# Key-maxima units of a gated attention kernel: four single PSUM banks each, 92 instead of 76 of them in the front

## The chip, the core and the metric

The kernel runs on one core of one Trainium2 chip. TensorE (PE in the profile) multiplies matrices into PSUM, a memory of eight banks of 128 partitions by 512 fp32 values. ScalarE (ACT) and VectorE (DVE) read PSUM and SBUF, GpSimd (POOL) works on SBUF, and SyncE's queue (SP) issues the transfers. Each engine executes its own instructions in the order in which they are written, and waits on semaphores for the others. The metric is the device time of one execution in microseconds; the figure given is the median over runs.

## The reference

`x` is 2048 tokens of 448 features, 16 heads of 28. Branch A is a linear attention with learned softmax features, branch B a full softmax attention; a gate per token mixes them.

```python
def _A_ref(x, wqkv, w_phi, wo):
    qkv = (lambda x, *d: x.transpose(*d))((x @ wqkv).reshape(B, S, 3, H, Dh), 2, 0, 3, 1, 4)
    q, k, v = qkv[0], qkv[1], qkv[2]
    pq = jnp.einsum("bhsd,hdf->bhsf", q, w_phi)
    pk = jnp.einsum("bhsd,hdf->bhsf", k, w_phi)
    phi_q = jnp.concatenate([_softmax(pq, axis=-1), _softmax(-pq, axis=-1)], axis=-1)
    phi_k = jnp.concatenate([_softmax(pk, axis=-1), _softmax(-pk, axis=-1)], axis=-1)
    kv = jnp.einsum("bhsf,bhsd->bhfd", phi_k, v)
    z  = jnp.einsum("bhsf->bhf", phi_k)
    num = jnp.einsum("bhqf,bhfd->bhqd", phi_q, kv)
    den = jnp.einsum("bhqf,bhf->bhq", phi_q, z)[..., None] + 1e-6
    ...
def _B_ref(x, wqkv, wo):
    ...
    scores = jnp.einsum("bhqd,bhkd->bhqk", q, k) * scale
    p = _softmax(scores, axis=-1)
    o = jnp.einsum("bhqk,bhkd->bhqd", p, v)
    ...
g = _sigmoid((x * gate_w).sum(-1, keepdims=True))
return g * a + (1 - g) * b
```

## The kernel before

The kernel is one long program whose order on PE, DVE, ACT and POOL is the order of the Python code (`manual_schedule`, L52). It has two parts.

**The front** (up to about 360 us) computes the projections of both branches, all of branch A, and the values of branch B. After a first stretch of query and key projections (`first_units`, `proj_qk`), one loop (L712) runs over steps `i`, with `t = i` counting key tiles of 128 tokens of branch A for the first 16 steps, and `q = i - 16` counting query tiles and what follows them. A step with a key tile runs eleven matmuls of keys (`pk`), eleven of values (`pva`), the features (`features1`, `features2`: on DVE two reductions `ext`, the sum `fsum` and a reciprocal per tile; the exponential on ACT; subtractions and a multiplication on POOL) and every second step `kv_add` for two tiles, 32 small matmuls that the trace shows as 64. The steps from `q = 18` on (the value stage) run `value_b`, eleven matmuls `pvb` for 128 tokens of branch B's values, and `out_a`, twelve matmuls `poa`. After the loop, `value_b` runs on for value tiles 8 to 15 (L887).

**The attention** (L1129) takes 256 steps: a step is one block of 512 queries, one tile of 128 keys and four heads. Per step it runs four score matmuls `st` (L856), four exponentials `p` on ACT (L872), and eight matmuls `pv` of the values (L1000). Steps 1 to `first` go in pairs (n = 2), later ones up to `LAST` = 232 singly, then in pairs again.

**The maxima.** The softmax of branch B subtracts a bound, the greatest score of each query and head, which must be known before that query block's attention. The whole task is `NU` = 256 units of four matmuls. `NF` = 76 of them run in the front as `mx_unit`; the rest run in the attention as `mx_visit`, one per pair or per single step, so `first = 2 * (LAST - len(flats) // 4)` follows from `NF`: 180 visits are left, the first 104 steps go as 52 pairs with one visit each, and steps 105 to 232 have one visit each.

A front unit (L260) works on 128 queries, two heads and two blocks of 512 keys. Four matmuls of 28 rows, in the four row quarters of the array, make for each head scores of one block (into `pmb`) and the difference of the two blocks' scores (into `pmd`). The greater of two numbers is one plus the relu of their difference: ACT takes the relu of `pmd` (both heads, 128x1024) into `rl`, then DVE adds `pmb` to `rl` and takes the maximum, one instruction for each head (L291). `pmb` and `pmd` are tiles of two banks each. Their pool has four banks (`mx`, two buffers of two banks) until the loop ends; then a new layout (`psv`, L882) has two single banks for the projections and six for the units.

Where units stand in the front: four in the last projections (L669); in the key tiles one at the start of every second step (L718) and three more after counted matmuls (`pace`, `tick`, L704); one in each of the steps q = 0, 1 and from q = 8 on (L757); one more just ahead of `value_b` for 19 <= q < 26 (L803); the rest spread evenly over value tiles 8 to 14 (L891). The differences of key blocks that units need come with `pair_load` (SP transfers, then a subtraction on POOL, taken by `take_subs`).

Of the kernel before, what the change touches and what calls it, by code (L numbers as in the profile page):

```python
# [8 lines left out]
F32 = mybir.dt.float32  # L9
F32R = mybir.dt.float32r  # L10
U32 = mybir.dt.uint32
AF = mybir.ActivationFunctionType
ALU = mybir.AluOpType
# [13 lines left out]
SCALE = DH ** -0.5  # L27
EPS = 1e-6
NU = NG * NQ * 16
NF = 76  # L30
LOWEST = -3.0e38
LAST = 232
OUTS = (200, 238, 246, 206)
# [8 lines left out]
def gated_mix_kernel(ctx, tc, xT, wqkB, wvB, wvA, wkAT, wqAT, phi, woA, woB,  # L42
# [15 lines left out]
    ps = ps_s_.enter_context(tc.tile_pool(name="ps", bufs=1, space=PSUM, reuse_waits="tile"))  # L58
    dr = ctx.enter_context(tc.tile_pool(name="dr", bufs=1, space=DRAM))

    psn = [3, 2]

    def ps_s(nm):
        return ps.tile([P, 512], F32, tag="s", name=nm, bufs=psn[0])
# [1 line left out]
    def ps_pv(nm):  # L66
        return ps.tile([P, 512], F32, tag="pv", name=nm, bufs=1)

    def ps_mx(nm, d):
        return ps.tile([P, 2, 512], F32, tag="md" if d and psn[1] == 3 else "mx", name=nm,  # L70
                       bufs=1 if d and psn[1] == 3 else 2)


    def scratch(nm, shape):
# [185 lines left out]
    def mx_unit():  # L260

        u = mxs["u"]
        if u == NF:
            return
        mx_fin()
        take_diffs(2)
        mxs["u"] = u + 1
        gq, r = divmod(u, 16)
        g, qb = divmod(gq, NQ)
        if gq < GM:  # L270
            c, qt = divmod(r, 4)
            hp, b = divmod(c, 2)
            col = 64 * gq + 16 * b + 4 * qt + 2 * hp
            if r in (4, 9):
                pair_query(gq + 1, r // 9)
        else:
            c, qt = divmod(r, QM)
            hp, b = divmod(c, 2)
            col = 64 * gq + 4 * QM * b + 4 * qt + 2 * hp
            if r == 0:  # L280
                mx_query(gq)
        qc, kc = mxs[("qp", gq, hp)], mxs[("kp", g, c)]
        pb, pd = ps_mx(f"pmb{u}", False), ps_mx(f"pmd{u}", True)
        for j in range(4):
            js = slice(32 * j, 32 * j + DH)
            nc.tensor.matmul((pb if j < 2 else pd)[:, j % 2, :], qc[js, qt * P:(qt + 1) * P],  # L286
                             kc[js, :], start=True, stop=True, tile_position=(32 * j, 0))
        rl = rlp.tile([P, 2, 512], F32, tag="rl", name=f"rl{u}", bufs=2 if psn[1] == 3 else 1)
        nc.scalar.activation(rl, pd, AF.Relu)  # L289
        for i in range(2):  # L290
            nc.vector.tensor_tensor_reduce(rl[:, i, :], pb[:, i, :], rl[:, i, :], 1.0, LOWEST,  # L291
                                           ALU.add, ALU.max, part[:, col + i:col + i + 1])
        if gq < GM and qt == 3 and qb == NQ - 1:
            pair_load(g + 1, c)
        if gq == GM and qt == QM - 1:
            mx_load(g, c)
        if r == 15:
            mx_reduce(gq)
# [312 lines left out]
    def first_units():  # L611
# [5 lines left out]
            nc.sync.dma_start(raw[b][:, 1, :], xT[:, b, :512])  # L617
        x_loads(1)
        pqs = [ps_s(f"pqk0_{m}") for m in range(3)] + [ps_pv("pqk0_3")]
        pr = [ps_mx(f"pqk_{i}", False) for i in range(2)]  # L620
        later.extend((pr[0][:, 0, :], pr[1][:, 0, :], pr[0][:, 1, :]))
        for _ in range(8):
            nc.tensor.matmul(pqs[3][:, :P], ident, ident, start=True, stop=True)
        for b in range(4):
# [87 lines left out]
    for i in range(2 * NT + 11):  # L712
# [4 lines left out]
        if t < NT and t % 2 == 0:  # L717
            mx_unit()  # L718
            passes = (55 if t < NT - 4 else 44) + (4 if t >= 4 else 0)
            pace["n"], pace["at"] = 4 if t >= 4 else 0, [k * passes // 4 for k in (1, 2, 3)]  # L720
        if q in (0, 1):
            take_exps()

# [40 lines left out]
        if 2 <= q - 1 < NT:  # L764
            fq[q - 1] = features2(fq[q - 1], f"q{q - 1}")
        take_subs()
        if t == 1:
            pair_load(0, 3)
        if y >= 8 and y % 2 == 0 and tb - 4 < 8:
            num[tb - 4] = normalize3(*num[tb - 4], 2)  # L770
# [30 lines left out]
            turn(y - 2)  # L801
        if NT + 3 <= q < NT + 10:
            mx_unit()  # L803
        if q == NT + 2:
            bd_s.close()
            vb = [value_tile(0)]
        if 0 <= q - NT - 2 < 8:
            value_b(q - NT - 2)
        if y >= 5 and y % 2 and tb - 2 < 8:
            num[tb - 2] = normalize2(ta, *num[tb - 2], f"a{tb - 2}", 2, True)  # L810
    ta_s.close()
# [38 lines left out]
    def scores(s, i, js=range(4)):  # L850

        gq, kt = divmod(s, NT)
        g, qb = divmod(gq, NQ)

        def score(j, st):
            nc.tensor.matmul(st, kst_of[(g, kt // 4)][:, j, (kt % 4) * P:(kt % 4 + 1) * P],  # L856
                             qst_of[gq][:, j, :], start=True, stop=True)

        if s == 0:
            p = at.tile([P, 2, 512], F32, name=f"p{s}_{i}")  # L860
            st = ps_mx(f"st{s}_{i}", i)
            for jl in range(2):
                score(2 * i + jl, st[:, jl, :])
            nc.scalar.activation(p, st, AF.Exp, scale=SCALE)
            pts.setdefault(s, []).extend([p[:, 0, :], p[:, 1, :]])
            return
        sts = {j: bank(b, f"st{s}_{j}") for j, b in zip(js, i)}
        for j in js:
            score(j, sts[j])
        for j in js:  # L870
            p = late_p.tile([P, 512], F32, tag="p", name=f"p{s}_{j}", bufs=12)
            nc.scalar.activation(p, sts[j], AF.Exp, scale=SCALE)  # L872
            pts.setdefault(s, []).append(p)
# [4 lines left out]
    stg = at  # L878
    load_q(0)
    load_nm(0)  # L880
    ps_s_.close()
    ps = ps_s_.enter_context(tc.tile_pool(name="psv", bufs=1, space=PSUM, reuse_waits="tile"))  # L882
    psn[:] = 2, 3
    rlp = fr_s.enter_context(tc.tile_pool(name="rlp", bufs=1, reuse_waits="tile"))
    mx_unit()
    rest = NF - mxs["u"]
# [26 lines left out]
        return ps2.tile([P, 512], F32, tag=f"g{i}", name=nm, bufs=1)  # L913


    for i in (3, 4, 1, 2, 5, 6, 0, None):
        if i is None:
            ps2.tile([P, 512], F32, tag="pv", name="pv_first", bufs=1)
        else:
            bank(i, f"first{i}")  # L920
# [331 lines left out]
```

## Time and profile before

| | before |
|---|---|
| median of 3 runs (lowest, highest) | 1015.66 us (1015.43, 1016.14) |
| profiled execution, its own time | 1016.56 us |
| span of its trace | 1014.8 us |
| front, from 0 to the first attention matmul | 360.0 us |
| attention in pairs, first visit to last pair's visit | 366.5 to 593.8 us |
| attention singly | 593.8 to 924.4 us |
| granted TensorE clock | 1.000 |

Times in the trace are microseconds from the start of the span. In a timeline a row gives the start, the length from the first start to the last end of like instructions that follow each other, the engine, the line, the operation, output <- inputs, the shape, and how many there were. PE's ends are modelled and overlap, so the distance between starts on PE is read rather than the lengths. L110, L128 and L286 are the lines that issue projection and unit matmuls.

### The profile page before, as it was taken

What the parts mean: (1) busy time and instruction counts of PE and PEld (TensorE: products, weight loads), DVE (VectorE), ACT (ScalarE), POOL (GpSimd) and SP (SyncE); (2) the same over time, 40 slices, a digit from 0 to 9 for tenths busy, and PEclk for the clock granted to TensorE, in tenths of its full rate; (3) what the DMA queues carried; (4) which work ended last, traced back from release to release, by engine and by line L of the source; (5) the groups of instructions that cost most, each with busy time, mean ns of one, the idle gap of its engine ahead of it and who ended that gap; (6) DMA issues with size and microseconds to landing.
All of it is one profiled execution on the core that took longest, in us unless ns stands there. A gap on an engine that the chain in (4) does not pass through costs nothing.

```text
span 1014.8 us, 17693 instructions
## 1 busy us (share of the span) xinstructions
PE 1004.8 (99%) x6344; PEld 566.7 (56%) x6344; DVE 647.5 (64%) x1335; ACT 818.1 (81%) x1534; POOL 250.9 (25%) x218
## 2 busy tenths in 40 slices
PE   8999999999999999999999999999999999999998
PEld 7777877777777754444444443333333333335665
DVE  5467767898765535445444568888888788885112
ACT  5355655577765699999999999999999999997662
POOL 1225435578734820220110120110110101100010
PEclk9999999999999999999999999999999999999999
DMA  8874010113233671223542233342232247310441
GB/s 294 289 250 120 33 52 31 43 37 95 84 97 98 153 164 38 58 66 74 112 96 72 71 90 81 79 105 56 73 85 61 71 98 200 96 38 30 136 145 55
DMA packets 64570, 99.62 MB, mean 98 GB/s; under 512 B 18134, under 2 KB 24902, under 8 KB 64482
## 3 DMA queue, kind: packets, MB, share of 16 engines
q1 hardware_dynamic: 64482, 98.49, 35.8%
q8 instruction: 50, 0.82, 0.4%
q14 instruction: 38, 0.31, 0.1%
HBM read 70.29 MB, written 27.78 MB: 97 GB/s over the span
## 4 chain that ended last, share of the span: by engine, by line
PE 95%; DVE 3%; ACT 1%; DMA 1%; issue 0%; POOL 0%; DVEq 0%; ACTq 0%; POOLq 0%
PE st L856 28%; PE pv L1000 24%; PE pm L323 8%; PE pqk L110 5%; PE poa L110 4%; PE pk L128 4%; PE pva L128 4%; PE pmb L286 3%; PE pob L110 3%; PE pq L110 2%; PE pvb L110 2%; PE pvb L128 2%; PE pn L538 1%; PE pqk L640 1%; PE pft L526 1%; DVE featq L453 1%
## 5 line engine op out<-in xcount | busy, mean ns | idle before, releaser
L872 ACT ACTIVATE p<-st 128x512 f32<-128x512 f32 x1020 | 525.1, 639 | 26.4 <-PE st L856 26.4
L335 DVE TENSOR_REDUCE part<-pm 128x1 f32<-128x512 f32 x405 | 258.8, 685 | 178.7 <-PE pm L323 178.7
L856 PE MATMUL st<-qst,kst 128*128 128x512 f32 x1024 | 299.5, 422 | 0.1
L1000 PE MATMUL pv<-p,vb 128*32 128x512 f32 x2048 | 259.7, 601 | 0.0
L856 PEld LDWEIGHTS st<-qst,kst 128*128 128x128 f32 x1024 | 171.0, 187 | 101.6 <-ACT p L872 39.3
L425 POOL TENSOR_TENSOR oUb<-oUb,rsb 128x512 f32<-128x512 f32 x15 | 19.3, 1289 | 492.4 <-DMA rsb<-rdb 360.1
L291 DVE CUSTOM_DVE_ANT_0 rl<-pmb,rl 128x512 f32<-128x512 f32 x152 | 98.3, 684 | 57.0 <-ACT rl L289 57.0
L327 ACT ACTIVATE rl<-pm 128x512 f32<-128x512 f32 x180 | 111.5, 620 | 10.4 <-PE pm L323 10.0
L323 PEld LDWEIGHTS pm<-kc,qc 28*128 28x128 f32 x720 | 34.4, 181 | 150.9 <-ACT p L872 102.3
L289 ACT ACTIVATE rl<-pmd 128x1024 f32<-128x1024 f32 x76 | 78.1, 1028 | 38.2 <-PE pmd L286 31.0
L1000 PEld LDWEIGHTS pv<-p,vb 128*32 128x32 f32 x2048 | 50.5, 108 | 96.0 <-issue 93.6
L332 DVE CUSTOM_DVE_ANT_0 rl<-pm,rl 128x512 f32<-128x512 f32 x135 | 92.0, 681 | 0.0
L323 PE MATMUL pm<-kc,qc 28*128 28x512 f32 x720 | 91.2, 495 | 0.0
L110 PE MATMUL pqk<-XH,wB 128*128 128x512 f32 x192 | 59.6, 397 | 1.7 <-DVE ev L578 1.7
L577 ACT CAST ev<-pqk 128x512 fp32r<-128x512 f32 x28 | 15.9, 588 | 36.7 <-PE pqk L110 32.0
L110 PE MATMUL poa<-woA_s,oTa 128*128 128x448 f32 x192 | 43.4, 375 | 0.0
L110 PEld LDWEIGHTS pqk<-XH,wB 128*128 128x128 f32 x192 | 35.3, 188 | 10.6 <-DVE ev L578 2.2
L1011 DVE SCALAR_TENSOR_TENSOR acc<-pob,gate,acc 128x448 f32<-128x448 f32 x12 | 8.2, 684 | 50.8 <-PE pob L110 50.8
L128 PE MATMUL pk<-wkA_s,XH 128*128 128x448 f32 x128 | 39.5, 382 | 0.0
L286 PE MATMUL pmd<-kp,qp 28*128 28x512 f32 x152 | 38.0, 496 | 0.8 <-DVE part L291 0.8
L110 PEld LDWEIGHTS poa<-woA_s,oTa 128*128 128x128 f32 x192 | 34.9, 188 | 6.2 <-issue 3.2
L128 PE MATMUL pva<-wvA_s,XH 128*128 128x450 f32 x128 | 37.8, 371 | 0.0
(155 smaller groups left out, 1196.1 us busy)
## 6 DMA issues: line engine op xcount, KB each, us to landing
qkd<-ev SPq DMA_DIRECT2D x28, 512.0 KB
qst<-qkd SPq DMA_DIRECT2D x64, 224.0 KB
kst<-qkd SPq DMA_DIRECT2D x64, 224.0 KB
od<-oTb SPq DMA_DIRECT2D x48, 112.0 KB
rsa<-rda SPq DMA_DIRECT2D x8, 512.0 KB
rsb<-rdb SPq DMA_DIRECT2D x15, 256.0 KB
gad<-ga SPq DMA_DIRECT2D x16, 224.0 KB
acc<-gad SPq DMA_DIRECT2D x4, 896.0 KB
```

What stands on the lines that cost most here:

```text
L110: nc.tensor.matmul(dst, l, r, start=i == 0, stop=i == len(todo) - 1)
L128: nc.tensor.matmul(dst[:, :n], l, r, start=i == 0, stop=i == len(todo) - 1, skip_group_check=True)
L286: nc.tensor.matmul((pb if j < 2 else pd)[:, j % 2, :], qc[js, qt * P:(qt + 1) * P], kc[js, :], start=True, stop=True, tile_position=(32 * ...
L289: nc.scalar.activation(rl, pd, AF.Relu)
L291: nc.vector.tensor_tensor_reduce(rl[:, i, :], pb[:, i, :], rl[:, i, :], 1.0, LOWEST, ALU.add, ALU.max, part[:, col + i:col + i + 1])
L323: nc.tensor.matmul(pm[j], mxs[("qc", gq)][js, qt * P:(qt + 1) * P], mxs[("kc", g, kb)][js, :], start=True, stop=True, tile_position=(32 * ...
L327: nc.scalar.activation(rl, pm[kb], AF.Relu if kb < 3 else AF.Copy)
L332: nc.vector.tensor_tensor_reduce(r, pm[j], r, 1.0, LOWEST, ALU.add, ALU.max, part[:, col + j:col + j + 1])
L335: nc.vector.tensor_reduce(part[:, col + j:col + j + 1], pm[j], AX.X, ALU.max)
L856: nc.tensor.matmul(st, kst_of[(g, kt // 4)][:, j, (kt % 4) * P:(kt % 4 + 1) * P], qst_of[gq][:, j, :], start=True, stop=True)
L872: nc.scalar.activation(p, sts[j], AF.Exp, scale=SCALE)
L1000: nc.tensor.matmul(pv[32 * j:32 * j + 32, :], vb[kt // 8][:, kt % 8, 4 * g + j, :], pt[j], start=kt == 0, stop=kt == NT - 1, tile_position ...
```

## The change

A unit takes four single banks in place of two tiles of two, all from one tag `mx` with four buffers (six in the later layout). The matmuls of the differences are issued first, then those of the scores. Each head has its own relu of 128x512 and its own `rl` tile, and its DVE instruction follows. The pace in the key tiles asks for five places to two key tiles (matmul counts at fifths, not quarters). A third unit comes inside `value_b` for 19 <= q < 26, ahead of its sixth matmul. The layout `psv` is opened in step q = 22 (`NT + 6`), not after the loop. `NF` is 92. The load of the fourth pair of key blocks moves from step 1 to step 0. The first attention step takes four single banks and four exponentials of 128x512, and the order in which the attention's banks are laid out at its start is another one.

```diff
-NF = 76
+NF = 92
...
-    psn = [3, 2]
+    psn = [3, 4, 2]
...
-    def ps_mx(nm, d):
-        return ps.tile([P, 2, 512], F32, tag="md" if d and psn[1] == 3 else "mx", name=nm,
-                       bufs=1 if d and psn[1] == 3 else 2)
+    def ps_mx(nm):
+        return ps.tile([P, 512], F32, tag="mx", name=nm, bufs=psn[1])
...
-        pb, pd = ps_mx(f"pmb{u}", False), ps_mx(f"pmd{u}", True)
+
+        pm = [ps_mx(f"pm{'ddbb'[j]}{u}_{j % 2}") for j in range(4)]
         for j in range(4):
-            js = slice(32 * j, 32 * j + DH)
-            nc.tensor.matmul((pb if j < 2 else pd)[:, j % 2, :], qc[js, qt * P:(qt + 1) * P],
-                             kc[js, :], start=True, stop=True, tile_position=(32 * j, 0))
-        rl = rlp.tile([P, 2, 512], F32, tag="rl", name=f"rl{u}", bufs=2 if psn[1] == 3 else 1)
-        nc.scalar.activation(rl, pd, AF.Relu)
+            i = (j + 2) % 4
+            js = slice(32 * i, 32 * i + DH)
+            nc.tensor.matmul(pm[j], qc[js, qt * P:(qt + 1) * P], kc[js, :], start=True, stop=True,
+                             tile_position=(32 * i, 0))
         for i in range(2):
-            nc.vector.tensor_tensor_reduce(rl[:, i, :], pb[:, i, :], rl[:, i, :], 1.0, LOWEST,
-                                           ALU.add, ALU.max, part[:, col + i:col + i + 1])
+            rl = rlp.tile([P, 512], F32, tag="rl", name=f"rl{u}_{i}", bufs=psn[2])
+            nc.scalar.activation(rl, pm[i], AF.Relu)
+            nc.vector.tensor_tensor_reduce(rl, pm[2 + i], rl, 1.0, LOWEST, ALU.add, ALU.max,
+                                           part[:, col + i:col + i + 1])
...
-            pace["n"], pace["at"] = 4 if t >= 4 else 0, [k * passes // 4 for k in (1, 2, 3)]
+            pace["n"], pace["at"] = 4 if t >= 4 else 0, [k * passes // 5 for k in range(1, 5)]
...
-        if t == 1:
+        if t == 0:
             pair_load(0, 3)
...
+        if q == NT + 6:
+            ps_s_.close()
+            ps = ps_s_.enter_context(tc.tile_pool(name="psv", bufs=1, space=PSUM, reuse_waits="tile"))
+            psn[:2] = 2, 6
...
-            value_b(q - NT - 2)
+            value_b(q - NT - 2, lambda i: mx_unit() if i == 5 and q >= NT + 3 else None)
...
-            p = at.tile([P, 2, 512], F32, name=f"p{s}_{i}")
-            st = ps_mx(f"st{s}_{i}", i)
-            for jl in range(2):
-                score(2 * i + jl, st[:, jl, :])
-            nc.scalar.activation(p, st, AF.Exp, scale=SCALE)
-            pts.setdefault(s, []).extend([p[:, 0, :], p[:, 1, :]])
+            for j in (2 * i, 2 * i + 1):
+                p, st = at.tile([P, 512], F32, name=f"p{s}_{j}"), ps_mx(f"st{s}_{j}")
+                score(j, st)
+                nc.scalar.activation(p, st, AF.Exp, scale=SCALE)
+                pts.setdefault(s, []).append(p)
...
-    ps_s_.close()
-    ps = ps_s_.enter_context(tc.tile_pool(name="psv", bufs=1, space=PSUM, reuse_waits="tile"))
-    psn[:] = 2, 3
...
-    for i in (3, 4, 1, 2, 5, 6, 0, None):
+    for i in (0, None, 1, 6, 5, 4, 3, 2):
```

More of the change, by code (lines that the diff above doesn't have):

```diff
@@ L619, in first_units @@
         pqs = [ps_s(f"pqk0_{m}") for m in range(3)] + [ps_pv("pqk0_3")]
-        pr = [ps_mx(f"pqk_{i}", False) for i in range(2)]
-        later.extend((pr[0][:, 0, :], pr[1][:, 0, :], pr[0][:, 1, :]))
+        later.extend(ps_mx(f"pqk_{i}") for i in range(3))
         for _ in range(8):
```

## The prediction

> **What bounds the kernel now.** I read the page's busy line and chain first.
>
> ```profile
> span 1014.8 us, 17693 instructions
> PE 1004.8 (99%) x6344; PEld 566.7 (56%) x6344; DVE 647.5 (64%) x1335; ACT 818.1 (81%) x1534; POOL 250.9 (25%) x218
> PE 95%; DVE 3%; ACT 1%; DMA 1%; issue 0%; POOL 0%; DVEq 0%; ACTq 0%; POOLq 0%
> ```
>
> PE sets the end nearly everywhere, so a unit moved from the attention to the front isn't hidden in idle time: it is paid there and saved here, and the two prices have to be compared. They come from the stages. The busy times by window, the first over the paired steps (from the first pair's visit to the last pair's), the second over the single ones:
>
> ```profile
> core 0: us, PE busy (x) PEld busy (x) DVE busy (x) ACT busy (x) POOL busy (x), PEclk, DMA share, GB/s
> 366.53:593.85 227.32, 227.32 (x1436) 104.37 (x1432) 109.41 (x222) 227.16 (x461) 25.62 (x26) 1.00 0.35 80
> 593.85:924.40 330.55, 330.55 (x2048) 126.82 (x2048) 270.41 (x544) 320.36 (x642) 31.80 (x29) 1.00 0.35 84
> ```
>
> 51 periods of a pair lie in the first, 227.3/51 = 4.457 us each; ACT is busy throughout, so the pairs run at the pace of ACT. The second holds 128 single steps (2048 matmuls, 16 each), 330.55/128 = 2.582 us each; ACT has 10 us of slack there, and PE sets the pace. ACT's own timeline shows the price of a pair, one relu and eight exponentials without a gap, 4.45 us from relu to relu:
>
> ```profile
> 469.69 0.60 ACT L327 ACTIVATE rl<-pm 128x512 f32<-128x512 f32 x1
> 470.18 4.02 ACT L872 ACTIVATE p<-st 128x512 f32<-128x512 f32 x8
> 474.14 0.60 ACT L327 ACTIVATE rl<-pm 128x512 f32<-128x512 f32 x1
> ```
>
> **Saved in the attention.** With `NF` = 92 there are 164 visits, not 180, and `first` is 136, not 104. So 32 single steps with 32 visits become 16 pairs with 16 visits: each takes 4.457 in place of 2 x 2.582 = 5.164 us, 0.707 less, times 16: **-11.3 us**. The maxima still come in time: the block of queries 9 is finished with visit 68, at step 136, and its load stands at step 140; before, block 7 was finished at 104 and its load stood at 108.
>
> **Paid in the front.** PE's price of a unit, by starts on PE in the value tiles after the loop, where nothing else stands between the matmuls:
>
> ```profile
> 286.07 0.37 PE L110 MATMUL pvb<-wvB_s,XL 128*128 128x448 f32 x1
> ...
> 286.69 0.37 PE L110 MATMUL pvb<-wvB_s,XL 128*128 128x448 f32 x1
> ...
> 337.82 0.49 PE L286 MATMUL pmb<-kp,qp 28*128 28x512 f32 x2
> ...
> 338.25 0.67 PE L128 MATMUL pvb<-wvB_s,XH 128*128 128x448 f32 x2
> ...
> 358.44 0.50 PE L286 MATMUL pmb<-kp,qp 28*128 28x512 f32 x2
> ```
>
> Three matmuls of a projection take 0.62 us without a unit, 0.207 each. From unit 65 (337.82) to unit 75 (358.44) run ten units and 70 such matmuls: 20.62 - 70 x 0.207 = 6.13, so 0.613 a unit. That is more than the 0.43 us from a unit's first start to the projection behind it (337.82 to 338.25); the matmuls on both sides of it also start late. 16 units: **+9.8 us**. By placing: six in the key tiles (four pairs of tiles from t = 4 and the two from t = 12; in the first two pairs the count, 44 ticks from 0, never reaches the fourth place, 44, so they keep four units), seven inside `value_b`, three more after the loop (14, not 11).
>
> Without waits the change would be worth -1.5 us. The waits decide.
>
> **Waits at units, now.** A unit's relu, its two DVE instructions, and the next unit that takes the banks, in the value stage:
>
> ```profile
> 323.68 0.50 PE L286 MATMUL pmb<-kp,qp 28*128 28x512 f32 x2
> ...
> 324.32 1.02 ACT L289 ACTIVATE rl<-pmd 128x1024 f32<-128x1024 f32 x1
> ...
> 325.37 0.69 DVE L291 CUSTOM_DVE_ANT_0 rl<-pmb,rl 128x512 f32<-128x512 f32 x1 [1.81 <-ACT rl L289]
> ...
> 325.99 0.69 DVE L291 CUSTOM_DVE_ANT_0 rl<-pmb,rl 128x512 f32<-128x512 f32 x1
> ...
> 326.58 0.49 PE L286 MATMUL pmb<-kp,qp 28*128 28x512 f32 x2
> 326.60 0.09 DVE L291 DVE_READ_ACCUMULATOR2_ANT part<- 128x1 f32 x1
> ...
> 326.74 0.50 PE L286 MATMUL pmd<-kp,qp 28*128 28x512 f32 x2
> ```
>
> From the start of a unit to the end of its DVE work 326.69 - 323.68 = 3.0 us go by; the next unit stands 2.9 us later, and half of it waits, 0.16 us. Such splits stand at seven units of the value stage, 1.2 us in all. With single banks the first relu lasts 0.60 (the row at 469.69), not 1.02, so the DVE work ends 0.4 earlier, 2.59 us after the unit's start: these splits go, **-1.2 us** (at least 0, if ACT's queue delays the relus).
>
> The fourth bank of a unit is still freed by the second DVE instruction of the unit ahead, as long as there are four banks. So the new places count: how far apart are they?
>
> *In the value stage*, the new unit stands five matmuls behind the one ahead of `value_b`: 5 x 0.207 + 0.613 = 1.65 us. Its fourth bank comes after 2.59 + 0.05 (the 326.69 to 326.74 above), so PE waits 0.99 us. This holds for q = 19 to 21 and, since the changed program still has the unit of q = 22 wait for DVE after the layout is swapped, for q = 22: four times, **+4.0 us**. From q = 23 on six banks rotate, and a unit's last bank waits for the second relu of the unit ahead: 324.32 - 323.68 + 0.49 (relu to exponential, 469.69 to 470.18) + 0.60 + 0.05 = 1.78, so 0.13 each of three. After the loop, units stand 5 and 6 matmuls apart, 1.65 and 1.85 us, some 0.1 each of seven: together **+1.0 us** (0 to 2). What is behind the waiting unit on PE is the rest of `pvb` and then `poa`, so it is all on the path.
>
> *In the last four key tiles* the DVE reductions of the features stand ahead of a unit's DVE work:
>
> ```profile
> 164.82 0.61 DVE L448 TENSOR_REDUCE extk<-pck 128x16 f32<-128x448 f32 x1
> 165.01 0.50 PE L286 MATMUL pmb<-kp,qp 28*128 28x512 f32 x2
> ...
> 165.36 0.61 DVE L449 TENSOR_REDUCE extk<-pck 128x16 f32<-128x448 f32 x1
> ...
> 165.62 1.03 ACT L289 ACTIVATE rl<-pmd 128x1024 f32<-128x1024 f32 x1 [0.79 <-PE pmd L286]
> 165.88 1.07 DVE L462 TENSOR_REDUCE fsumk<-featk 128x32 f32<-128x896 f32 x1
> ...
> 166.99 0.35 DVE L463 RECIPROCAL fsumk<-fsumk 128x32 f32<-128x32 f32 x1
> ...
> 167.26 0.63 DVE L291 CUSTOM_DVE_ANT_0 rl<-pmb,rl 128x512 f32<-128x512 f32 x1
> ...
> 168.09 0.50 PE L286 MATMUL pmb<-kp,qp 28*128 28x512 f32 x2
> 168.43 0.08 DVE L291 DVE_READ_ACCUMULATOR2_ANT part<- 128x1 f32 x1
> 168.56 0.50 PE L286 MATMUL pmd<-kp,qp 28*128 28x512 f32 x2
> ...
> 174.86 0.49 PE L286 MATMUL pmb<-kp,qp 28*128 28x512 f32 x2
> 175.50 0.50 PE L286 MATMUL pmd<-kp,qp 28*128 28x512 f32 x2 [0.15 <-DVE part L291]
> ...
> 181.64 0.49 PE L286 MATMUL pmb<-kp,qp 28*128 28x512 f32 x2
> 182.12 0.50 PE L286 MATMUL pmd<-kp,qp 28*128 28x512 f32 x2
> ```
>
> Here 3.5 us pass (165.01 to 168.51); the next unit stands 3.1 us later and waits 0.47; with 0.64 and 0.48 at the other two that makes 1.6 us. A shorter relu doesn't help, since the reciprocal ends after it (167.34 against 166.65). Five units to two tiles stand 9 or 10 matmuls apart, 2.5 to 2.7 us, and two of five meet these reductions (a tile has one such run): 0.9 to 1.2 us each, four times, 4.2 us in place of 1.6: **+2.6 us**. At most all ten units wait 0.9, +7; at least nothing is added.
>
> *In the key tiles before*, units will stand 12 matmuls apart, 12 x 0.207 + 0.613 = 3.1 us, where 14 or 15 make 3.5 to 3.7. Following the order of the changed program with these durations, the unit after the one that meets `fsum` is about 0.2 late, once in each of four pairs: **+0.8 us** (0 to 3).
>
> *In the last projections*, the changed program gives unit 2 one bank twice: its fourth matmul takes the bank of its own first, and waits for its own relu.
>
> ```profile
> 59.80 0.50 PE L286 MATMUL pmb<-kp,qp 28*128 28x512 f32 x2
> ...
> 60.41 1.03 ACT L289 ACTIVATE rl<-pmd 128x1024 f32<-128x1024 f32 x1
> ```
>
> The relu starts 0.61 after the unit and lasts 0.60, plus 0.05: **+1.25 us** (0 if ACT is earlier). The program does the same in three units of the last four key tiles (35, 37, 40); there the bank that it avoids would be as late, so nothing is added for them.
>
> At nothing I take: the second relu instruction on ACT (it runs while DVE takes the first), the earlier load of the fourth pair (first used by unit 12, which stays at t = 4), the POOL subtractions of the next group's blocks, which come five steps earlier, and the start of the attention, whose first two pairs wait for exponentials of the same total length. Each could be -0.5 to +1.
>
> **The sum.** -11.3 + 9.8 - 1.2 + 4.0 + 1.0 + 2.6 + 0.8 + 1.25 = **+6.9 us**. The span of 1014.8 becomes 1021.7, its execution, 1.8 longer than its span, 1023.5 where it was 1016.56; that execution lies 0.9 over the median, so the median is forecast at 1015.66 + 6.9 = **1022.6 us**.
>
> **Rivals.** *The finer banks dissolve the waits* (faster). Each bank comes back alone, the unit's first two need only relus, and if the fourth is never late, the 1.2 and 1.6 us of present waits go and no new ones come: -11.3 + 9.8 - 2.8 = -4.3, 1011.4. For it: each split above waits only for DVE's last instruction. Against: that instruction frees the fourth bank still, and 1.65 us is less than relu and two DVE instructions take. [...]
>
> *The gain is given back exactly* (same): the new unit inside `value_b` waits half as long, because the relus overlap the matmuls of their own unit (2.0 in place of 4.0), unit 2 doesn't wait (-1.25), and the key tiles keep their 1.6 (-2.6): 6.9 - 5.85 = +1.0, 1016.7.
>
> *DVE becomes the bound of the key tiles* (slower still). For two tiles, by the rows above, features take 2 x (0.61 + 0.61 + 1.07 + 0.35) = 5.3 and five units 5 x 1.3 = 6.5 us (325.37 to 326.69), of a period of 13 to 16; if every run of reductions makes the next unit wait 3.5 - 3.1 + 0.2 = 0.6, that is eight in the four earlier pairs, 4.8 in place of 0.8, +4.0: 1026.6.
>
> [...]
>
> *The saving doesn't come*, because the pairs of steps 105 to 136 go slower than the first 52: +11.3 at most, 1033.9. Against it, the rate of 51 pairs is even.
>
> **How the numbers follow.** The forecast has 0.50 (its own range 1018.5 to 1025), the slower DVE case 0.18, the same 0.13, the dissolved waits 0.14, the lost saving 0.02; 0.03 for something faster that I don't see. A measurement of this kernel tells about 0.2%, 2.0 us, from no change: 1013.6 to 1017.7. Faster 0.17, same 0.13, slower 0.70. The range from 1013.8 to 1028.0 holds all but the faster cases and the lost saving.
>
> **What would show it.** Paired steps to 136 at 4.46 us, single ones from there at 2.58. Unit starts in the value stage whose fourth matmul comes about 1 us after the first at the unit inside `pvb`, four times, and hardly ever after the swap. In the last four key tiles four to five such splits of about 1 us, in the tiles before few over 0.3. Unit 2 split by 1.2 us. If those four splits are missing, the largest wait of my sum is wrong, and with it the sign may be.

## The result and the profile after

The changed kernel takes 1027.19 us (median of 4, 1025.84 to 1028.31) where the kernel before takes 1015.90 on the same chip: the ratio is 1.0108, with a 95% interval of 1.0089 to 1.0127. It is slower. The forecast was 1022.6 us; the time lies inside the range and 2.2 us above the likeliest case's own range.

The profiled execution took 1028.31 us. Its page:

```profile
span 1026.5 us, 18068 instructions
PE 1012.1 (99%) x6344; PEld 575.0 (56%) x6344; DVE 635.0 (62%) x1335; ACT 829.4 (81%) x1628; POOL 251.0 (24%) x218
PE 92%; DVE 3%; issue 1%; DMA 1%; ACT 1%; SPq 1%; POOL 0%; DVEq 0%; ACTq 0%; POOLq 0%
```

The number of matmuls is that of before, 6344, and PE still sets the end, but its share of the chain has gone from 95 to 92%, and issue and the SP queue have come in with 1% each. The span has grown by 11.7 us. The first attention matmul, at 360.01 before, is now at 378.74: the front is 18.7 us longer. From there to the end it was 654.7 and is now 647.8: the attention is 7.0 shorter.

The busy times by window, after: the pairs up to one that stands out, that one pair, the pairs behind it, the single steps, and 3.5 us near the start. The columns are those of before.

```profile
core 0: us, PE busy (x) PEld busy (x) DVE busy (x) ACT busy (x) POOL busy (x), PEclk, DMA share, GB/s
385.15:554.54 169.39, 169.39 (x1068) 77.74 (x1065) 81.50 (x166) 169.24 (x344) 23.77 (x24) 1.00 0.38 85
554.54:563.81 9.27, 6.08 (x32) 2.54 (x29) 1.90 (x4) 5.16 (x11) 0.00 (x0) 0.82 0.48 112
563.81:688.48 124.67, 124.67 (x789) 57.33 (x785) 60.60 (x122) 124.06 (x252) 9.54 (x9) 1.00 0.33 77
688.48:936.56 248.08, 248.08 (x1540) 95.36 (x1536) 202.83 (x408) 240.43 (x482) 24.16 (x22) 1.00 0.35 84
36.80:40.30 3.50, 3.48 (x13) 3.11 (x14) 1.74 (x3) 0.53 (x1) 1.16 (x9) 0.52 0.74 270
```

There are 38 pairs in the first window and 28 in the third, 294.06/66 = 4.455 us each, and 96 single steps of 248.08/96 = 2.584 in the fourth: the prices that the prediction used, and so the saving of 11.3 us is there. One pair takes 9.27 us in place of 4.46 and gives 4.8 of it back. Two stretches run at a lower granted clock, the long pair and the 3.5 us at 37 us; the kernel before had no such stretch in its profiled execution ahead of its last 0.6 us, where PE is done (the last section says how this differs between executions).

**The long pair.** The timeline around it (SPq rows are the issues of SP's queue, with the time that the queue spent on them):

```profile
532.45 6.03 SPq L176 DMA_DIRECT2D kc<-qkd  x8
538.59 0.36 SPq L419 DMA_DIRECT2D rdb<-denb  x1
...
540.23 0.60 SPq L420 DMA_DIRECT2D rsb<-rdb  x1
...
548.94 1.28 POOL L426 TENSOR_TENSOR oUb<-oUb,rsb 128x512 f32<-128x512 f32 x1 [8.85 <-DMA rsb<-rdb]
...
552.29 3.40 SPq L1057 DMA_DIRECT2D od<-oTb  x4
...
554.98 1.25 PE L860 MATMUL st<-qst,kst 128*128 128x512 f32 x4
555.73 2.47 SPq L846 DMA_DIRECT2D qst<-nm  x4
...
559.42 2.05 PE L860 MATMUL st<-qst,kst 128*128 128x512 f32 x4 [3.19 <-DMA qc<-qkd]
```

Read it from the bottom. The scores of the next query block need the block's bounds in `qst`, a load (`qst<-nm`, L846) that is issued at 555.73, when PE is already at the block's first step. In SP's queue the load stands behind four stores of the finished block (`od<-oTb`, 552.29), and it is issued 0.04 us after the queue is done with them (552.29 + 3.40 = 555.69). The stores wait for POOL's normalisation, which waited 8.85 us for `rsb`; and `rsb` was issued late, at 540.23, because eight loads for the units' next heads (`kc<-qkd`, 6.03 us of the queue, 3.1 of them waits of the loads themselves) stand ahead of it and of `rdb`. The other block ends of the trace bear this out: there `rdb` is issued 0.28 us after the start of DVE's reciprocal (463.36 and 463.64, 499.03 and 499.31), here 3.89 us after it (534.70 and 538.59). From the issue of `rsb` to POOL's start it then takes 8.7 us, where the other ends have 5.5 and 7.8; why this is longer too isn't shown. With 92 units in the front the visits run ahead of the steps by 32 more, so that this change of heads falls on a block's end. PE's row names the load `qc` as its releaser; `qc` is only the one that landed near that time, as the first experiment shows. That experiment moves the bounds ahead of the stores; the loads for the next heads were not moved in any run, so their part rests on the comparison of block ends.

**Units in the front.** The unit in the last projections, one in the last key tiles with the DVE work that it waits for, and one inside `value_b`, each with what is behind it on PE:

```profile
61.09 0.50 PE L287 MATMUL pmd<-kp,qp 28*128 28x512 f32 x2
61.09 0.49 PE L287 MATMUL pmb<-kp,qp 28*128 28x512 f32 x1
62.28 0.49 PE L287 MATMUL pmb<-kp,qp 28*128 28x512 f32 x1 [0.69 <-ACT rl L291]
...
178.24 1.07 DVE L463 TENSOR_REDUCE fsumk<-featk 128x32 f32<-128x896 f32 x1
179.34 0.50 PE L287 MATMUL pmd<-kp,qp 28*128 28x512 f32 x2
179.62 0.63 DVE L292 CUSTOM_DVE_ANT_0 rl<-pmb,rl 128x512 f32<-128x512 f32 x1
180.31 0.49 PE L287 MATMUL pmb<-kp,qp 28*128 28x512 f32 x1 [0.46 <-DVE part L292]
181.00 0.50 PE L287 MATMUL pmb<-kp,qp 28*128 28x512 f32 x1 [0.20 <-ACT rl L291]
...
303.30 0.69 DVE L292 CUSTOM_DVE_ANT_0 rl<-pmb,rl 128x512 f32<-128x512 f32 x1 [1.92 <-ACT rl L291]
303.69 0.61 PE L287 MATMUL pmd<-kp,qp 28*128 28x512 f32 x2
303.92 0.69 DVE L292 CUSTOM_DVE_ANT_0 rl<-pmb,rl 128x512 f32<-128x512 f32 x1
304.05 1.11 PE L287 MATMUL pmb<-kp,qp 28*128 28x512 f32 x2
305.09 0.47 PE L127 MATMUL pvb<-wvB_s,XL 128*128 128x448 f32 x1
...
340.82 0.50 PE L287 MATMUL pmd<-kp,qp 28*128 28x512 f32 x2
340.82 0.66 PE L287 MATMUL pmb<-kp,qp 28*128 28x512 f32 x2
```

Call the time from the first start of a unit to its fourth its split. Unit 2 is split by 1.19 us. The unit at 179.34 is split by 1.66: `fsum` holds DVE until 179.31, then come the two DVE instructions of the unit ahead. The unit at 303.69 in the value stage starts when DVE has just taken up its predecessor, and gets its last bank at 304.67, 0.98 later. After the swap to six banks (340.82) it is 0.16. All splits of over 0.1 us in the front add up to 13.0 us, against 4.4 before.

**The first 40 us.** ACT's evictions and PE after:

```profile
34.23 1.04 ACT L368 CAST XH<-xraw 128x1024 fp32r<-128x1024 f32 x1 [6.93 <-DMA xraw<-in_xT_dram]
35.18 1.55 ACT L578 CAST ev<-pqk 128x512 fp32r<-128x512 f32 x3
...
36.82 1.92 PE L394 MATMUL pwk<-phi_s,wtk 112*128 112x112 f32 x8 [3.63 <-issue]
```

ACT waits 6.93 us for a block of `x`, and three evictions of projections stand behind that cast. PE has filled its three banks and waits 3.63 us; its row names no releaser, and e9 below shows that the evictions behind the cast are what it waits for. In the kernel before, PE had already waited 1.75 us at 21 us for an eviction, when three projections still shared two-bank tiles; it reached the place ahead of the fold later and waited only 1.44 us there:

```profile
22.96 0.73 PE L110 MATMUL pqk<-XH,wB 128*128 128x512 f32 x2 [1.75 <-DVE ev L578]
...
37.15 1.12 PE L393 MATMUL pwk<-phi_s,wtk 112*128 112x112 f32 x8 [1.44 <-issue]
```

The wait at 21 us goes with the tiles: e8 below, which has them, shows it too (2.16), and no profile of a run with single banks does. The fold `pwk`, the product that follows the projections here, starts at about the same time in both (37.15 and 36.82). But the one long wait is followed by 3.4 us at half the granted clock (0.52 from 36.80 to 40.30, the last row of the windows).

### The profile page after: what moved, and what is told of

It is laid out like the page before. It is cut to its first block, busy times and chain, and to the rows that moved or that the text cites. A ratio compares the mean times of both kernels' runs of the same rounds, so it can differ in the third digit from the quotient of the medians.

```text
span 1026.5 us, 18068 instructions
## 1 busy us (share of the span) xinstructions
PE 1012.1 (99%) x6344; PEld 575.0 (56%) x6344; DVE 635.0 (62%) x1335; ACT 829.4 (81%) x1628; POOL 251.0 (24%) x218
## 4 chain that ended last, share of the span: by engine, by line
PE 92%; DVE 3%; issue 1%; DMA 1%; ACT 1%; SPq 1%; POOL 0%; DVEq 0%; ACTq 0%; POOLq 0%
PE st L860 27%; PE pv L1000 23%; PE pm L324 7%; PE pqk L109 6%; PE pk L127 4%; PE pvb L127 4%; PE poa L109 4%; PE pmd L287 3%; PE pva L127 3%; PE pob L109 3%; PE pq L109 3%; PE pn L539 1%; PE pft L527 1%; PE pqk L640 1%; DVE rl L292 1%
## 5 line engine op out<-in xcount | busy, mean ns | idle before, releaser
L336 DVE TENSOR_REDUCE part<-pm 128x1 f32<-128x512 f32 x369 | 235.9, 686 | 206.8 <-PE pm L324 206.8
L292 DVE CUSTOM_DVE_ANT_0 rl<-pmb,rl 128x512 f32<-128x512 f32 x184 | 118.8, 682 | 45.0 <-ACT rl L291 44.6
L291 ACT ACTIVATE rl<-pmd 128x512 f32<-128x512 f32 x184 | 100.9, 601 | 33.5 <-PE pmb L287 25.7
L328 ACT ACTIVATE rl<-pm 128x512 f32<-128x512 f32 x164 | 101.0, 616 | 9.9 <-PE pm L324 9.0
L324 PEld LDWEIGHTS pm<-kc,qc 28*128 28x128 f32 x656 | 31.4, 181 | 137.5 <-ACT p L875 78.0
L333 DVE CUSTOM_DVE_ANT_0 rl<-pm,rl 128x512 f32<-128x512 f32 x123 | 83.8, 681 | 0.0
L324 PE MATMUL pm<-kc,qc 28*128 28x512 f32 x656 | 83.0, 495 | 0.0
L287 PE MATMUL pmb<-kp,qp 28*128 28x512 f32 x184 | 52.6, 494 | 2.7 <-ACT rl L291 1.3
L287 PE MATMUL pmd<-kp,qp 28*128 28x512 f32 x184 | 46.6, 496 | 0.0
```

The source lines that it names most:

```text
L287: nc.tensor.matmul(pm[j], qc[js, qt * P:(qt + 1) * P], kc[js, :], start=True, stop=True, tile_position=(32 * i, 0))
L291: nc.scalar.activation(rl, pm[i], AF.Relu)
L292: nc.vector.tensor_tensor_reduce(rl, pm[2 + i], rl, 1.0, LOWEST, ALU.add, ALU.max, part[:, col + i:col + i + 1])
L324: nc.tensor.matmul(pm[j], mxs[("qc", gq)][js, qt * P:(qt + 1) * P], mxs[("kc", g, kb)][js, :], start=True, stop=True, tile_position=(32 * ...
L328: nc.scalar.activation(rl, pm[kb], AF.Relu if kb < 3 else AF.Copy)
L333: nc.vector.tensor_tensor_reduce(r, pm[j], r, 1.0, LOWEST, ALU.add, ALU.max, part[:, col + j:col + j + 1])
```

## The experiments

Each run is compared with the kernel before on its own chip (1015.73 to 1015.95 us).

| run | units | what it is | median us (lowest to highest) | ratio, 95% interval |
|---|---|---|---|---|
| e1_nm | 92 | the change, block 5's bounds loaded early | 1023.99 (1022.98 to 1025.24) | 1.0061 to 1.0092 |
| e2_swap | 92 | e1, six banks from q = 19 | 1022.11 (1021.92 to 1022.72) | 1.0043 to 1.0073 |
| e3_tail | 92 | e1, four units to two of the last key tiles | 1019.58 (1018.86 to 1020.82) | 1.0020 to 1.0046 |
| e4_tags | 92 | e1, a bank of its own for each matmul of a unit | 1022.58 (1021.69 to 1023.62) | 1.0047 to 1.0077 |
| e5_best92 | 92 | e1 to e4 together, and two places more | 1015.76 (1011.99 to 1016.76) | 0.9976 to 0.9998 |
| e6_banks76 | 76 | single banks alone | 1017.04 (1014.00 to 1019.43) | 0.9994 to 1.0017 |
| e7_banks76t | 76 | e6 with e4's banks | 1015.81 (1013.42 to 1019.17) | 0.9987 to 1.0011 |
| e8_units | 92 | the new units alone, two-bank tiles | 1038.35 (1037.38 to 1040.60) | 1.0200 to 1.0238 |
| e9_late92 | 92 | e5, a later cast of `x` | 1010.99 (1010.06 to 1012.20) | 0.9939 to 0.9964 |
| e10_late76 | 76 | e7, a later cast, two early loads | 1009.87 (1009.73 to 1010.46) | 0.9929 to 0.9954 |
| e11_late1 | 92 | e1, a later cast | 1020.58 (1019.43 to 1021.38) | 1.0031 to 1.0059 |
| e12_latebef | 76 | the kernel before, a later cast | 1015.47 (1013.29 to 1016.79) | 0.9986 to 1.0004 |

**e1: is the long pair SP's order?** The bounds of block 5 are loaded at key tile 7, ahead of the stores.

```diff
-            if kt == (12 if gq + 1 < 14 else 14) and gq + 1 < NG * NQ - 1:
+            if kt == (7 if gq == 4 else 12 if gq + 1 < 14 else 14) and gq + 1 < NG * NQ - 1:
```

> The changed kernel with one load moved: the bounds of query block 5 (qst<-nm) are issued ahead of the four transfers od<-oTb in SP's queue, not behind them. Theory A (SP's queue): the 9.27 us pair at 554 us of the changed kernel comes from those od transfers, which wait for GpSimd, which waits for rsb<-rdb, and hold up qst<-nm behind them; then the pair is back at 4.45, and the span is 4.8 us less than the 1026.5 of the profiled run, 1021.7. Rival B (transfers are late because the DMA engines are full of the next heads' keys): the pair stays over 8 us wherever the load stands. Rival C: the stall only moves to the next block's load, same span. The front is unchanged: first attention matmul at 378.7.

SP's queue in this run:

```profile
546.34 4.32 SPq L846 DMA_DIRECT2D qst<-nm  x4
550.76 3.42 SPq L1057 DMA_DIRECT2D od<-oTb  x4
```

The load now goes first, no pair is long any more, the span falls from 1026.5 to 1021.5 (-5.1), and the median by 3.2. The load of `qc`, which the row of PE had named, is issued at 554.23, still behind the stores, and PE doesn't wait: it wasn't the cause. e2 to e5, e8, e9 and e11 keep this repair, and e10 has it for one block more; e6, e7 and e12 don't have it.

**e2, e3, e4: the three groups of splits, one at a time.** e2 swaps to six banks ahead of the first unit inside `value_b` (condition `q == NT + 3`, placed above that unit, in place of `NT + 6`). e3 gives the last four key tiles four places to two tiles as before, with the units left over after the loop. e4 names a bank for each of the four matmuls:

```diff
-            pace["n"], pace["at"] = 4 if t >= 4 else 0, [k * passes // 5 for k in range(1, 5)]
+            pace["n"], pace["at"] = 4 if t >= 4 else 0, [k * passes // (5 if t < NT - 4 else 4)
+                                                                   for k in range(1, 5 if t < NT - 4 else 4)]
```

```diff
-    def ps_mx(nm):
+    def ps_mx(nm, j=None):
+        if j is not None and psn[1] == 4:
+            return ps.tile([P, 512], F32, tag=f"mx{j}", name=nm, bufs=1)
...
-        pm = [ps_mx(f"pm{'ddbb'[j]}{u}_{j % 2}") for j in range(4)]
+        pm = [ps_mx(f"pm{'ddbb'[j]}{u}_{j % 2}", j) for j in range(4)]
```

> As e1_nm, and the layout with six banks is opened in step q = 19, not 22. Theory: the four splits of 1 us at the unit inside value_b come from having four banks; three of them shrink to 0.16 (the first still waits for DVE across the swap), so the front ends 2.6 us earlier, first attention matmul at 376.1, and the whole is 2.6 less than e1_nm. Rival: DVE itself is the limit of three units per value tile; then the wait goes to the next unit and less than 1 us is gained.

> As e1_nm, and the last four key tiles keep four units to two tiles; the two units go to the value tiles after the loop (16 there, not 14). Theory: the waits of 4.6 us in those key tiles (0.47, 1.26, 1.65, 1.26) come from units 2.6 us apart behind the features' DVE reductions; at 3.1 us apart they are what they were before, 1.6 us (three of about 0.5), less where the first relu decides; 16 units after the loop stand 4 to 5 matmuls apart, 1.45 to 1.65 us, and wait 0.1 to 0.35 each, 2 us more there. Net about -1 us against e1_nm. Rival: the waits are of the four banks and not of the distance; then they stay at 4 us and the net is +1 to +2.

> As e1_nm, and each of a unit's four matmuls has a bank of its own while there are four, so that none waits for its own unit's relu. Theory: unit 2 loses its wait of 1.19 us; units 35, 37 and 40 wait for DVE instead, about as long (1.26, 1.65, 1.26, within 0.3). The whole is 1.2 us less than e1_nm. Rival: those three, too, lose most of their wait, and the whole is 4 to 5 us less.

e2: three splits of 1.02 us go to 0.16, but one of 0.73 appears at a unit further on, where DVE has waited for a transfer of branch A's normalisation. That leaves 1.85 of the 2.6 expected, and the median falls by 1.88. (The span falls by only 1.24, because in this profiled execution unit 2, which the edit doesn't touch, already stands 0.47 later: 61.00 and 60.53.) The mechanism holds and some 0.7 us of its worth comes back as a wait further on.

e3: the unit that was split by 1.66 is now at

```profile
179.42 0.50 PE L287 MATMUL pmd<-kp,qp 28*128 28x512 f32 x2
179.43 0.50 PE L287 MATMUL pmb<-kp,qp 28*128 28x512 f32 x2
```

and all four of its group are whole. The span falls by 3.65, not by the 1 expected: with single banks and four units to two tiles, the 1.6 us of waits that the kernel before had at this place are gone as well. Behind the loop, where 16 units stand now, not 14, four are split by 0.2 to 0.4.

e4: unit 2 is whole, and the unit at 171 us still split:

```profile
60.67 0.50 PE L289 MATMUL pmd<-kp,qp 28*128 28x512 f32 x2
60.68 0.50 PE L289 MATMUL pmb<-kp,qp 28*128 28x512 f32 x2
...
171.09 0.50 PE L289 MATMUL pmd<-kp,qp 28*128 28x512 f32 x2
171.67 1.11 PE L289 MATMUL pmb<-kp,qp 28*128 28x512 f32 x2
```

The unit's wait for its own relu was 1.19 us at unit 2 and only 0.08 at each of the three in the last key tiles, where the other bank is nearly as late; both as forecast. The span falls by 1.27.

**e5 to e8: banks alone, units alone, all repairs.** e6 and e7 take the change with `NF` = 76, quarters in the pace, no unit inside `value_b` and the load of the fourth pair back in step 1. e8 takes the two-bank tiles, the layouts and the fourth pair's load of before with `NF` = 92, the fifths and the unit inside `value_b` (and e1's load). e5 goes beyond e1 to e4 in two places: the first four key tiles have their places at quarters again too, and the swap stands ahead of the first unit of step q = 19.

> All repairs at once, still 92 units: the bounds of block 5 ahead of od in SP's queue; one bank for each of a unit's matmuls while there are four; the layout of six banks from step q = 19 and ahead of that step's unit; five places to two key tiles only for t = 4 to 11, four in the first and in the last four; 16 units after the loop. Theory (the loss is waits at units and one SP stall, and a unit moved is worth 0.707 - 0.61 us): waits of about 3.8 us stay (units 4 and 45 0.8 each, seven of 0.16, a few of 0.2 to 0.4 after the loop), first attention matmul at 360.0 - 4.4 + 9.8 + 3.8 = 369.2, the attention 11.6 shorter than before's as in e1_nm, span 1012.4, 2.4 under before's 1014.75. Rival (waits removed in one place come back at the next, as in e2_swap, which gained 1.4 of 2.6): half of the 9 us of waits returns, first attention matmul at 373 to 374, span 1016 to 1017.

> The single banks and the layouts of the changed kernel, with the 76 units where they stood before. Theory: the banks alone help, since the first relu ends 0.4 us earlier: the seven splits of the value stage (1.2 us) and the three of the last key tiles (1.6, as e3_tail shows) go, and unit 2 waits for its own relu (+1.2): span 1014.75 - 2.8 + 1.2 = 1013.1. Rival: the finer banks themselves cost (184 relus of 0.60 in place of 76 of 1.03 on ScalarE), span over 1016.

> As e6_banks76, with one bank for each of a unit's matmuls while there are four. Theory: unit 2 no longer waits, span 1014.75 - 2.8 = 1011.9, 0.28% under before. Rival: as in e6_banks76.

> The kernel before, with its two tiles of two banks for a unit, and 92 units placed as in the changed kernel (layout of six banks after the loop, as before), the bounds of block 5 loaded early as in e1_nm. Theory: a relu of 1.03 makes a unit's banks free after 3.0 us, so all seven units inside value_b wait 3.05 - 1.65 = 1.4 us, 9.8 in all, the last key tiles 4 to 5, some 2.5 elsewhere: first attention matmul at 360.0 - 4.4 + 9.8 + 16.8 = 382, span 1025. So the units cost, and the banks take some of it back (e1_nm has 1021.5). Rival: the fine banks are what costs; then it is at or under 1017.

e8 shows what the finer banks are for. A unit inside `value_b` and the next one:

```profile
313.91 0.50 PE L286 MATMUL pmb<-kp,qp 28*128 28x512 f32 x2
315.26 0.50 PE L286 MATMUL pmd<-kp,qp 28*128 28x512 f32 x2 [0.85 <-DVE part L291]
...
317.14 0.49 PE L286 MATMUL pmb<-kp,qp 28*128 28x512 f32 x2
318.27 0.50 PE L286 MATMUL pmd<-kp,qp 28*128 28x512 f32 x2 [0.64 <-DVE part L291]
```

Splits of 1.35 at seven such units, and 1.13 to 1.21 at the units behind them, 28.6 us in the whole front: the new units on the old tiles are 22.4 us slower than before, and single banks, with the six of them from q = 22, take 14.4 of that back (1038.35 to 1023.99). I had expected a span of 1025, and it is 1036.5; 8.2 of these 11.5 us are the seven units behind, which I had not counted.

e6 and e7 say that single banks at 76 units are worth nothing in the median, although their splits fall from 4.4 to 2.9 and 1.8 us and the attention starts 1.5 and 4.5 earlier. (They have 152 relus in the front, two for each of 76 units, not the 184 of e6's expectation.) e7 shows where it went: a long pair of 7.88 us at block 4, again the bounds behind the stores, with 1.79 us of idle PE and 3.4 us at half clock. The attention runs earlier and its chain of transfers hardly does: at this block's end DVE's reciprocal starts 4.66 us earlier than before (475.79 and 480.45), the stores only 1.91 (491.30 and 493.21). e5, with all repairs, reaches the kernel before and no more; its PE waits 4.36 us at 33 us, followed by 6.8 us at half clock.

**e9 to e12: the wait in the first 40 us.** The last block of `x` is split two projections later, behind the evictions that it held up.

```diff
-        if n % 4 == 1 and n < 12:
+        if n in (1, 5, 11):
             split_x(n // 4 + 1, raws.pop(("x", n // 4 + 1)))
```

e9 is e5 with this, e10 is e7 with this and with the bounds of blocks 4 and 5 at key tile 7, e11 is e1 with this, e12 the kernel before with this.

> The kernel with all repairs and 92 units, and one move more: the split of the fourth block of x (two casts on ScalarE behind the load that lands at about 34 us) is issued two projections later, so that the evictions of the projections are no longer queued behind it on ScalarE. Theory (TensorE's one long idle stretch ahead of the fold, 4.36 us at 33 to 37 us, is a wait for a bank whose eviction stands behind that cast, and it is what lowers the granted clock to 0.5 for the 6.8 us after it): idle and clock drop both go, the clock is 1.0 from start to end, and the span falls from 1015.0 by up to 4.4 + 3.4, to about 1008 (1007 to 1010), if no later wait for a load takes the time back. Rival (the wait is for the load of the folded weights, which no move on ScalarE changes): the idle stays at about 4 us, the clock drops as before and the span stays at 1015.

> The kernel with the new banks, 76 units and a bank of its own for each matmul, with two moves: the same later split of the fourth block of x, and the query rows of blocks 4 and 5 loaded at key tile 7 of the block before. Theory: the idle of 2.3 us at 34 to 36 us goes, and so do the long pair of 7.88 us at 496 us and the half clock behind it (3.4 us in all), which takes the span from 1013.7 to about 1008 (1007 to 1010). With this the finer banks would be worth 6 to 7 us against the kernel before at the same 76 units, where they measured nothing; it would then be level with the 92-unit kernel of the same moves, so that the 16 units more would bring nothing. Rival (what the finer banks save is given back at whatever load comes next, wherever it is): the span stays within 1 us of 1013.7.

> The changed kernel with the query rows of block 5 loaded early (1023.99 measured, span 1021.45) and the later split of the fourth block of x alone. Theory (the idle of 3.4 us at 33 us and the 3.4 us at half clock behind it are part of what the change lost): the span falls by 3.4 + 1.7 to about 1016.4, and the first attention matmul from 378.35 to about 373.3. Rival (the kernel before had the same loss there, merely in two pieces, so that a later split brings no more than its 1.4): the span falls to about 1020.

> The kernel before with the later split of the fourth block of x alone: a control for what the move is worth without the change. Its own wait ahead of the fold is 1.44 us and its clock stays at 1.0 throughout, so by the theory the span falls from 1014.8 by 1.4 at most, to about 1013.4; were the move worth as much here as in the changed kernel (3 to 5 us), the clock drop would be no part of what the change lost.

e9's clock is 1.0 to its end, the idle is 0.87, the span 1009.4: -5.6, where up to 7.8 was expected. e10 reads

```profile
span 1008.0 us, 18033 instructions
PE 1001.1 (99%) x6344; PEld 564.8 (56%) x6344; DVE 648.4 (64%) x1335; ACT 821.2 (81%) x1612; POOL 250.6 (25%) x218
```

-5.7 against e7, as expected: with both obstacles out of the way the finer banks at 76 units are worth 5.9 us against the kernel before (1009.87 to 1015.73). In the profiles e10's attention starts 6.8 us earlier than that of before. Of this 3.5 us are there at unit 2 already (56.26 and 59.80): some 2.0 from the wait at 21 us that goes with the two-bank tiles, 0.4 around the fold, and 1.1 because this execution's projections come earlier from the start. The splits are another 2.6. The early loads alone were not tried on the kernel before; its pairs are even, so they have no long pair to remove there. e10 is the fastest version here; e9's interval overlaps its own.

e11 falls by 2.6 where 5.1 was expected. Its early idle is gone, but in the profiled execution the half clock is not; it stands at a later place. Two of the four executions (1019.43 and 1020.48) have a mean granted clock of 1.000, so this drop doesn't come each time. The windows of e11 and of e12 at their stretches of lower clock:

```profile
176.00:182.00 6.00, 5.80 (x79) 4.00 (x80) 2.38 (x7) 2.27 (x4) 1.19 (x1) 0.72 0.01 3
```

```profile
23.40:26.80 3.40, 3.31 (x8) 2.63 (x9) 0.73 (x2) 0.59 (x1) 0.00 (x0) 0.52 0.79 254
```

In e12 the 1.44 us at the fold are gone, but the wait at 21 us has grown from 1.75 to 2.77, behind it the clock is at half for 3.4 us, and the span is 0.2 longer than before. (Six of its eleven executions have a mean granted clock of 0.999, too high for 3.4 us at half of a span of 1015, and a median of 1014.8; the kernel before at a mean of 1.000 has 1015.0.) So the later cast alone is worth nothing that the runs can tell to the kernel before (0.9986 to 1.0004), 3.4 to e1 and 4.8 to e5.

## Why the prediction was nearly right, and what it lacked

*The saving of 11.3* held: 4.455 and 2.584 against 4.457 and 2.582.

*The price of 16 units, 9.8*, held. e9 and e10 have single banks, a bank for each matmul and the later cast in common. They differ in units, in the places for these, in the step of the swap (q = 19 and 22) and in e10's one more early load. The attention starts 13.07 us later in e9 (366.26 and 353.19). 1.8 of this are splits, and 1.07 stand ahead of all units that differ. Unit 2 in e9 and in e10:

```profile
57.33 0.50 PE L289 MATMUL pmd<-kp,qp 28*128 28x512 f32 x2
56.26 0.50 PE L289 MATMUL pmd<-kp,qp 28*128 28x512 f32 x2
```

The two programs are the same up to there, and the projections of the one execution stand later than those of the other from the first 8 us on. That leaves 10.2, or 0.64 a unit where 0.613 was forecast. The attention from there is 11.6 shorter, so that without splits and without that start the move of units is worth some 1.4 us, as the prediction has it (1.5); the 1.8 us of splits that its places bring take this back, and in the medians e9 is 1.1 us above e10.

*The seven splits that go, 1.2,* went. *The four units inside `value_b`, 4.0:* 0.97 and three times 1.02, so 4.0. *After the swap and the loop, 1.0:* four times 0.16 and nothing after the loop, 0.65. *Unit 2, 1.25:* 1.19. With four banks for its four matmuls the unit at 303.69 is split by 0.98 us, with six the one at 340.82 by 0.16.

*The last four key tiles, 2.6:* splits of 0.47, 1.26, 1.65 and 1.26, 4.65 in place of 1.6, so 3.0. *The key tiles before, 0.8:* none there; in their place unit 10, in the first four tiles, is split by 0.72 and unit 6 by 0.21, which I had not looked at.

By these terms the front was to grow by 18.25 us, and it grew by 18.7; the splits were to grow by 8.45 and grew by 8.6. That is partly luck, since the terms of the key tiles are off one by one and make up for each other. The wait in the first 40 us and the half clock behind it were in no term: some 1.4 us by the clock (1.7 for 3.4 us at half speed, less 0.3 because the fold starts earlier), 1.29 by the starts of unit 2 (61.09 and 59.80). Short waits of the kernel before that went (0.57 at 206 us and 0.27 at 228) were in none either. With these, 18.7 - 8.6 - 1.3 + 0.8 leaves 9.6 for the 16 units, 0.60 each.

**The step that failed** is the sentence "At nothing I take", which has the earlier subtractions for the next heads at -0.5 to +1 and doesn't name the loads that feed them. No wait of PE goes back to the subtractions. The loads stand in SP's queue ahead of `rdb` and `rsb`, and through the normalisation, the stores and the bounds they reach PE: 4.8 us in the profiled execution, 3.2 in the median by e1. The prediction looked at when the differences are needed and not at what the moved loads are queued ahead of. With those 3.2 the forecast would have been 1025.8, the lowest of the four measured times.

*The rivals.* DVE as the bound of the key tiles, 1026.6, came nearest to the time, for another reason than the true one: the earlier key tiles that it prices have no splits. Dissolved waits did not come with four banks in turn. e9, with 92 units, a bank for each matmul, six banks from q = 19 and fewer places in the key tiles, has splits of 3.6 us in all and is at 1010.99, where that rival had 1011.4 for the change. That the times agree is in part chance: e9 has the later cast too, and e5 without it is at 1015.76. The rival in which the gain is given back exactly asked for half the wait inside `value_b`, none at unit 2 and the old 1.6 us in the last key tiles; 4.0, 1.19 and 4.65 us were measured. The saving that doesn't come is ruled out by the 4.455 us of a pair.

What stays open: why e11's clock falls between 176 and 182 us (0.72 in the mean there), and why the transfer of `rsb` took longer at the block end of the long pair.

## What to carry to other kernels

When work moves from one stage to another, ask for every transfer that it takes along what is queued behind it, on the issuing queue, and follow that to the engine that sets the end; here 6.03 us of loads for later work held up a store, a load behind the store, and PE, 4.8 us in the profiled execution. Give a group that rotates through banks more banks than it takes at once: with four for its four matmuls a unit here got its last one, which its predecessor's last reader frees, 0.98 us after its start, and with six 0.16. When a bottleneck engine gets faster ahead of a fixed landing time, its waits can come as one long one: here PE waited 1.75 and 1.44 us before and 3.63 at once after, and in these two profiles the clock fell to half behind the 3.63 and not behind the other two; compare both kernels with that wait repaired before you judge the change.

## What was not expected of the hardware

**Behind some idle times of PE stand 3.4 us at half the granted clock.** The windows of the changed kernel at its two drops, the waits and one stretch of half clock:

```profile
33.20:36.90 3.70, 0.08 (x1) 0.11 (x2) 1.56 (x3) 2.50 (x4) 1.54 (x1) 1.00 0.96 370
555.80:559.20 3.40, 0.43 (x2) 0.11 (x1) 1.21 (x4) 1.83 (x4) 0.00 (x0) 1.00 0.26 53
559.20:562.60 3.40, 3.18 (x12) 1.56 (x16) 0.00 (x0) 2.06 (x4) 0.00 (x0) 0.50 0.54 148
```

In the profiles here the stretches at 0.5 ahead of the program's end last 3.4 us, or 6.8 in e5. Idle times of 3.63 and 3.19 us (the changed kernel), 3.4 (e1), 4.36 (e5) and 2.77 (e12) were followed by one. Of the shorter ones, 1.79 us (e7 at 497) and 2.16 (e8 at 21) were, and 2.31 (e7 at 34), 1.75 and 1.44 (before) weren't; so the length alone doesn't decide.

Nor does the time for which PE was busy just ahead. The 3.41 us of the kernel before in which its wait of 1.75 us lies, with no drop behind them, then e7's last 3.4 us ahead of its drop and the drop itself:

```profile
20.98:24.39 3.41, 1.66 (x8) 1.21 (x7) 1.38 (x2) 1.17 (x2) 0.00 (x0) 1.00 0.99 376
495.50:498.90 3.40, 1.81 (x12) 0.86 (x8) 1.89 (x4) 3.22 (x7) 0.00 (x0) 1.00 0.22 42
498.90:502.30 3.40, 3.19 (x12) 1.56 (x16) 0.00 (x0) 2.06 (x4) 0.00 (x0) 0.50 0.87 195
```

PE was busy for 1.66 of 3.41 us ahead of no drop and for 1.81 of 3.40 ahead of e7's, and in the 6 us in which e11's drop lies (176 to 182, granted clock 0.72) it was busy for 5.80. What decides stays open.

A profile shows one execution, and the drops differ between executions. Of the 15 of the kernel before that stand beside e9 to e12, nine have a mean granted clock of 1.000 (median 1015.04 us) and six have 0.997 or 0.998 (median 1016.4 us). So what one profile has of the clock, here and in the runs above, need not hold for the median.
